# Score matmuls issued one by one, a work list for projections, and output tiles of the last head group moved forward, in a fused attention and gated-MLP kernel

## The chip, the cores and the metric

The kernel runs on one core of a Trainium2 chip. The metric is device time in microseconds (us) of one execution; lower is better. Executions agree within about 0.2%, so an effect of 1 us in 1309 needs both repeated timing and the trace of one profiled execution. I name the engines as the profile does: PE (TensorE), PEld (its weight loads), ACT (ScalarE), DVE (VectorE), POOL (GpSimd), SP (SyncE, which issues the DMAs).

## The reference, cut to what matters

```python
xn = layernorm(x)                                   # x: 2048 x 512
q  = (xn @ wq) split in 32 heads of 128             # 512 x 4096
p  = softmax(q @ k_cache.T * 128**-0.5)             # per head 2048 x 2048
s  = concat_heads(p @ v_cache) @ wo                 # 4096 x 512
g  = silu(((relu(xn @ W_gate)) * (xn @ W_up)) @ W_down)
return x + s * g                                    # bf16 in and out
```

## The kernel before

A *block* is one head and 512 queries; there are 128 blocks (32 heads x 4). A block has 8 *steps*. In a step PE makes two score tiles (keys x queries, 128 x 512), ACT takes the exponential of both in one instruction, and three steps later PE uses the result as weights of eight value matmuls (129 columns: 128 values and one column that sums the softmax denominator). PSUM holds three pairs of banks for scores and projections (the ring) and two accumulator banks for the values. After a block's last value matmul DVE normalises the two banks (the *norm*), and DMA transposes the result for the output projection.

In the first step of a block PE also makes one query projection for the next head and one *output tile*: a 128 x 512 tile of the output projection of the previous group of 4 heads. Output tiles are summed in `s_acc`; the last group's 16 *final tiles* come after the loop and go straight into the result.

```python
def emit_S_pair(gp):                     # two scores, then the exp
    ...
    s = ring_acquire()
    for tt in range(2):
        ins = pe.matmul(ps_r[:, 2 * s + tt, :], KT_sb[h % 2][:, t * 128:(t + 1) * 128],
                        QT_sb[h % 2][:, qs], start=True, stop=True)
    ...
def emit_norm_bank(b, bank, pvtok):
    ob = b % NON                                     # NON = 16 buffers, one group
    _wait(dve, pvtok)
    if bank == 0 and b % (G * QB) == 0 and g >= 1:
        _wait(dve, t_tok(g - 1))                     # all transposes of the group before
    ...                                              # 1 reciprocal, 2 scalings per bank
    sp.dma_start_transpose(OT_store[...], Onorm[ob][:, j, :])   # 4 per block
...
for step in range(LAG, TOTP + LAG):
    emit_S_pair(gp)                                  # step gp
    if pq == 0:
        emit_M(hq + 1, Qq, op_item)                  # projection and at most one output tile
    emit_PV_pair(gq)                                 # values of step gp - 3: 8 matmuls
while oproj_queue: ...                               # what is left of group 6
for n in range(NT):                                  # 16 final tiles of group 7
    if n == 0:
        _wait(pe, t_tok(gL))
    ...                                              # 4 matmuls
    dve.tensor_tensor(fin_tmp[fb][:], ps_r[:, bank, 0:D], g_sb[:, n, :], ALU.mult)
    dve.tensor_tensor(x_sb[:, n, :], x_sb[:, n, :], fin_tmp[fb][:], ALU.add)
    ...                                              # stores
```

The softmax here doesn't subtract the row's maximum and nothing guards it: scores larger than these inputs give would overflow.

Of the kernel before, what the change touches and what calls it, by code (L numbers as in the profile page):

```python
# [5 lines left out]
BF16 = mybir.dt.bfloat16  # L6
# [45 lines left out]
def bass_recurrent_scan__mha_block_cached__glu_gated_reglu__prompt_kernel(  # L52
# [18 lines left out]
    NQ = 512  # L71
# [32 lines left out]
    with ExitStack() as es:  # L104
# [9 lines left out]
        def newsem(unit=1):  # L114
            _cnt[0] += 1
            return _Sem(es.enter_context(nc.semaphore(f"sem{_cnt[0]}")), unit)
# [47 lines left out]
        sem_out = newsem(16)  # L164
        sem_pool = newsem()
# [28 lines left out]
        with nc.Block() as block:  # L194

            @block.tensor
            def _(_pe_eng):
# [298 lines left out]
                oproj_queue = []  # L496
                bcount = [0]
                OPROJ_DELAY = 2

# [5 lines left out]
                def emit_M(h_qp, Q_qp, op_item):  # L505
                    do_qp = h_qp is not None and h_qp < H and (h_qp, Q_qp) not in qt_ready
                    if not do_qp and op_item is None:
                        return
                    s = ring_acquire()
                    toks = []  # L510
                    if do_qp:
                        toks.append(emit_qp(h_qp, Q_qp, 2 * s))
                    if op_item is not None:
                        g_, n_ = op_item
                        toks.append(emit_oproj_tile(g_, n_, 2 * s + 1))
                    ring_tok[s] = toks
# [59 lines left out]
                def emit_S_pair(gp):  # L576
                    b, h, Q, p = blk_of(gp)
                    qs = slice(Q * NQ, (Q + 1) * NQ)
                    if p == 0:
                        if (h, Q) not in qt_ready:  # L580
                            emit_M(h, Q, None)
                        _wait(pe, qt_ready[(h, Q)])
                        if Q == 0:
                            _wait(pe, kt_tok(h))
                    s = ring_acquire()
                    ins = None
                    for tt in range(2):
                        t = 2 * p + tt
                        ins = pe.matmul(ps_r[:, 2 * s + tt, :], KT_sb[h % 2][:, t * 128:(t + 1) * 128],  # L589
                                        QT_sb[h % 2][:, qs], start=True, stop=True)  # L590
# [11 lines left out]
                def emit_norm_bank(b, bank, pvtok):  # L602
# [10 lines left out]
                    for jj in range(2):  # L613
# [7 lines left out]
                        )  # L621
                    _wait(sp, tok)
                    if bank == 0 and b % (G * QB) == 0 and g >= 2:
                        _wait(sp, opg_tok.get(g - 2))
                    for jj in range(2):
                        j = 2 * bank + jj
                        sem_t[g % 2].sig(
# [7 lines left out]
                def emit_PV_pair(gp):  # L635
# [3 lines left out]
                    if p == 0:  # L639
                        if gp == 0:  # L640
                            _wait(pe, tok_pool)
                        if Q == 0:
                            _wait(pe, v_tok(h))
                    pe.wait_ge(sem_exp.h, gp + 1)
                    for tt in range(2):
                        t = 2 * p + tt
                        for j in range(4):
                            bank = j // 2
                            if t == 0 and j % 2 == 0:
                                _wait(pe, norm_tok[b - 1][bank] if b >= 1 else acc_free[bank])  # L650
                            o_ap = ps_acc[:, bank, (j % 2) * 256:(j % 2) * 256 + VW]
                            ins = pe.matmul(o_ap, PT[pb][:, tt, j * 128:(j + 1) * 128], V_sb[vb][:, t, :],  # L652
                                            start=(t == 0 and j % 2 == 0), stop=(t == KT - 1 and j % 2 == 1))
                            if t == KT - 1 and j == 1:
                                tx = sem_pv.sig(ins)
                            if t == KT - 1 and j == 3:
                                ty = sem_pv.sig(ins)
                    if p == NP - 1:
# [6 lines left out]
                        g, hh = divmod(h, G)  # L665
                        if hh == G - 1 and Q == QB - 1 and g < NG - 1:
                            for n in range(NT):
                                oproj_queue.append((bcount[0] + OPROJ_DELAY, g, n))

# [5 lines left out]
                for Q in range(QB):  # L675
                    emit_M(0, Q, None)
                sp_head_start(0)
                for gp in range(LAG):
                    emit_S_pair(gp)
                emit_down(QB - 1, hlast)  # L680
                glu_done_tok = sem_g.cur()
                if NG == 1:
                    for n in range(NT):
                        base_done[n] = None

                for step in range(LAG, TOTP + LAG):
                    gp = step
                    if gp < TOTP:
                        b, h, Q, p = blk_of(gp)
                        if p == 0 and Q == 0:  # L690
                            sp_head_start(h)
                        emit_S_pair(gp)
                    gq = step - LAG
                    if gq >= 0:
                        bq, hq, Qq, pq = blk_of(gq)
                        if pq == 0:
                            bcount[0] += 1
                            op_item = None
                            if oproj_queue and oproj_queue[0][0] <= bcount[0]:
                                _, g_, n_ = oproj_queue.pop(0)  # L700
                                op_item = (g_, n_)
                            emit_M(hq + 1, Qq, op_item)
                        emit_PV_pair(gq)

                while oproj_queue:
                    _, g_, n_ = oproj_queue.pop(0)
                    emit_M(None, None, (g_, n_))
                gL = NG - 1
                NFT = len(fin_tmp)
                fin_free = [None] * NFT  # L710
                fin_tok = {}
                chunk_start = [0]
                cur_slot = [None, []]

                for n in range(NT):
                    fb = n % NFT
                    if n % 2 == 0:
                        s = ring_acquire()
                        slot_toks = []
                    bank = 2 * s + (n % 2)  # L720
                    if n == 0:
                        _wait(pe, t_tok(gL))
                        _wait(pe, wo_tok(gL))
                    ins = None
# [3 lines left out]
                    otok = sem_op.sig(ins)  # L728
                    _wait(dve, otok)
                    _wait(dve, fin_free[fb])  # L730
                    mtok = sem_opa.sig(dve.tensor_tensor(fin_tmp[fb][:], ps_r[:, bank, 0:D], g_sb[:, n, :], ALU.mult))  # L731
                    slot_toks.append(mtok)
                    ring_tok[s] = list(slot_toks)
                    _wait(dve, mtok)
                    if n == 0:
                        _wait(dve, base_done.get(NT - 1))
# [38 lines left out]
```

## Time and profile before

The kernel before took 1308.88 us (median of 3). These lines are from the page of its profiled execution: the span, PE's busy time, and the chain of waits that ended last.

```profile
span 1309.6 us, 27449 instructions
PE 1281.4 (98%) x11744; PEld 838.4 (64%) x11964; DVE 442.6 (34%) x1190; ACT 1000.7 (76%) x1107; POOL 11.5 (1%) x23
...
PE 93%; DVE 3%; issue 2%; DMA 1%; SPq 0%; ACTq 0%; DVEq 0%
```

PE is the bound nearly everywhere. "98% busy" alone would not show it, since ends of matmuls are modelled; start-to-start intervals of the trace do. Means over complete steps without a projection, between 345 and 1240 us, in ns:

| | two scores | eight values | step |
|---|---|---|---|
| before | 216.7, 215.8 | 56.7, 56.7, 56.7, 56.7, 60.8, 55.9, 56.7, 57.5 | 890.0 |

The next lines, of DVE's timeline, give the first reciprocal of a norm, thus the end of a block (start, duration, instruction, and in brackets the idle time before it and what ended it). They are blocks 122 to 127.

```profile
1239.68 0.17 DVE L610 RECIPROCAL rz_sb<-ps_acc 128x2 f32<-128x2 f32 x1 [4.43 <-PE ps_acc L652]
...
1248.52 0.17 DVE L610 RECIPROCAL rz_sb<-ps_acc 128x2 f32<-128x2 f32 x1 [4.43 <-PE ps_acc L652]
...
1256.79 0.17 DVE L610 RECIPROCAL rz_sb<-ps_acc 128x2 f32<-128x2 f32 x1 [4.68 <-PE ps_acc L652]
...
1265.06 0.17 DVE L610 RECIPROCAL rz_sb<-ps_acc 128x2 f32<-128x2 f32 x1 [4.68 <-PE ps_acc L652]
...
1273.32 0.17 DVE L610 RECIPROCAL rz_sb<-ps_acc 128x2 f32<-128x2 f32 x1 [4.68 <-PE ps_acc L652]
...
1280.30 0.17 DVE L610 RECIPROCAL rz_sb<-ps_acc 128x2 f32<-128x2 f32 x1 [3.39 <-PE ps_acc L652]
```

A full block takes 8.85 us: 8 x 0.890 plus 8 matmuls of 0.216. The last four have no projection (no next head). Blocks 124 to 126 take 8.27 us, although 8 x 0.890 + 4 x 0.216 is only 7.98: with so little between two blocks' values, PE waits for the norm. (Block 127 ends 6.98 us after block 126, because its last three steps have no scores to make.) The view of waits has it (waiter, what it waited for, total, times, longest).

```profile
PEld ps_acc L652 <- DVE Onorm L617: 6.1, 21, 0.5
```

The tail, first PE's timeline, then the busy times by window (stretch, length, then busy time and instructions of each engine, PE's granted clock, DMA share, GB/s), then DVE's last instructions:

```profile
1278.38 2.00 PE L652 MATMUL ps_acc<-V_sb,PT 128*128 128x129 bf16 x32
1280.43 0.81 PE L545 MATMUL ps_r<-Wo_sb,OT_store 128*128 128x512 bf16 x3
1287.25 11.58 PE L726 MATMUL ps_r<-Wo_sb,OT_store 128*128 128x512 bf16 x40 [6.01 <-issue]
```

```profile
1281.30:1287.20 5.90, 0.00 (x0) 0.00 (x0) 2.51 (x5) 0.00 (x0) 0.00 (x0) 0.91 0.10 22
1287.20:1293.20 6.00, 5.95 (x15) 2.20 (x16) 2.87 (x5) 0.00 (x0) 0.00 (x0) 0.52 0.00 0
1293.20:1307.60 14.40, 10.76 (x50) 4.70 (x48) 13.88 (x28) 0.00 (x0) 0.00 (x0) 0.96 0.39 132
```

```profile
1306.08 0.43 DVE L737 TENSOR_TENSOR x_sb<-x_sb,fin_tmp 128x512 bf16<-128x512 bf16 x1
1306.42 0.68 DVE L731 TENSOR_TENSOR fin_tmp<-ps_r,g_sb 128x512 bf16<-128x512 f32 x1
...
1307.14 0.42 DVE L737 TENSOR_TENSOR x_sb<-x_sb,fin_tmp 128x512 bf16<-128x512 bf16 x1
```

Three things follow one another: PE stands still for 6.01 us (the profile names no releaser, "issue", but the kernel waits there for the last head's DMA transposes, and the trace has the last of them landed at 1287.16), then it runs at about half clock (0.52) for 6 us, then DVE is busy 13.88 of 14.40 us at 1.06 us per tile. From the last value matmul's start (1280.16) to the end are 29.5 us.

### The profile page before, as it was taken

The numbers are of one execution on the slowest core, as the hardware profiler recorded it, in microseconds if no ns is written. First come the engines' busy times: TensorE is split into PE (matmuls) and PEld (weight loads), VectorE is DVE, ScalarE is ACT, GpSimd is POOL, SyncE is SP. The second block draws the span as 40 slices with busy tenths as digits, with TensorE's granted clock in tenths as the row PEclk, the third lists the DMA queues.
The fourth block names the chain that finished last, engine by engine and source line by source line (L and its number), as shares of the span: only waits on it lengthen the run. The fifth ranks groups of instructions, "written<-read, shape, count | busy, mean of one in ns | idle before, by whom it ended". The sixth has DMA issues, their size and how long they took to land.

```text
span 1309.6 us, 27449 instructions
## 1 busy us (share of the span) xinstructions
PE 1281.4 (98%) x11744; PEld 838.4 (64%) x11964; DVE 442.6 (34%) x1190; ACT 1000.7 (76%) x1107; POOL 11.5 (1%) x23
## 2 busy tenths in 40 slices
PE   9999999999999999999999999999999999999996
PEld 3444466666666666666666666666666666666663
DVE  6333322222332332233233233223323323344546
ACT  3322389998888888888888888888888888888880
POOL 2000000000000000000000000000000000000000
PEclk9999999999999999999999999999999999999998
DMA  8500112232222322232221222222223222212202
GB/s 254 116 1 1 21 37 51 46 61 41 45 51 53 70 51 52 53 68 53 52 52 40 57 42 51 52 70 53 52 52 69 51 53 53 50 44 43 48 18 70
DMA packets 251575, 71.82 MB, mean 55 GB/s; under 512 B 238400, under 2 KB 251456, under 8 KB 251456
## 3 DMA queue, kind: packets, MB, share of 16 engines
q1 hardware_dynamic: 250640, 69.55, 25.4%
q8 instruction: 95, 1.56, 0.5%
q10 hardware_dynamic: 816, 0.52, 0.1%
q14 instruction: 24, 0.20, 0.0%
HBM read 32.77 MB, written 2.10 MB: 27 GB/s over the span
## 4 chain that ended last, share of the span: by engine, by line
PE 93%; DVE 3%; issue 2%; DMA 1%; SPq 0%; ACTq 0%; DVEq 0%
PE ps_acc L652 36%; PE ps_r L589 32%; PE ps_r L524 7%; PE ps_r L545 7%; PE ps_r L423 4%; PE ps_r L419 4%; PE ps_acc L456 4%; DVE Onorm L617 2%; DVE fin_tmp L731 1%; DMA Wu_sb<-in_B_W_up_dram 1%; PE ps_r L726 0%; DVE rz_sb L610 0%; SPq L628 0%; DMA OT_store<-Onorm 0%; ACTq L224 0%
## 5 line engine op out<-in xcount | busy, mean ns | idle before, releaser
L597 ACT ACTIVATE PT<-ps_r 128x1024 bf16<-128x1024 f32 x1024 | 952.3, 1054 | 172.8 <-PE ps_r L589 172.8
L652 PEld LDWEIGHTS ps_acc<-V_sb,PT 128*128 128x128 bf16 x8192 | 551.8, 98 | 247.9 <-DVE Onorm L617 6.1
L652 PE MATMUL ps_acc<-V_sb,PT 128*128 128x129 bf16 x8192 | 640.3, 221 | 2.5 <-DVE Onorm L617 0.4
L589 PE MATMUL ps_r<-QT_sb,KT_sb 128*128 128x512 bf16 x1844 | 565.5, 379 | 10.6
L610 DVE RECIPROCAL rz_sb<-ps_acc 128x2 f32<-128x2 f32 x256 | 42.2, 165 | 736.9 <-PE ps_acc L652 710.6
L589 PEld LDWEIGHTS ps_r<-QT_sb,KT_sb 128*128 128x128 bf16 x2048 | 159.3, 98 | 1.1 <-DVE QT_sb L535 0.4
L617 DVE TENSOR_SCALAR Onorm<-ps_acc,rz_sb 128x128 bf16<-128x128 f32 x512 | 156.1, 347 | 9.2
L524 PE MATMUL ps_r<-xnT,Wq_sb 128*128 128x512 bf16 x511 | 130.8, 379 | 0.1
L545 PE MATMUL ps_r<-Wo_sb,OT_store 128*128 128x512 bf16 x447 | 114.8, 379 | 0.1
L524 PEld LDWEIGHTS ps_r<-xnT,Wq_sb 128*128 128x128 bf16 x512 | 50.1, 98 | 60.5
L535 DVE CAST QT_sb<-ps_r 128x512 bf16<-128x512 f32 x128 | 87.2, 681 | 0.7 <-PE ps_r L524 0.7
L545 PEld LDWEIGHTS ps_r<-Wo_sb,OT_store 128*128 128x128 bf16 x448 | 43.8, 98 | 52.6 <-DMA OT_store<-Onorm 0.2
L429 ACT ACTIVATE gr_sb<-ps_r 128x512 bf16<-128x512 f32 x56 | 33.4, 596 | 56.2 <-PE ps_r L419 53.5
L558 DVE TENSOR_TENSOR s_acc<-s_acc,ps_r 128x512 f32<-128x512 f32 x96 | 65.9, 687 | 12.3
L419 PE MATMUL ps_r<-xnT,Wg_sb 128*128 128x512 bf16 x220 | 57.7, 384 | 1.0 <-DMA Wu_sb<-in_B_W_up_dram 0.8
L423 PE MATMUL ps_r<-xnT,Wu_sb 128*128 128x512 bf16 x219 | 57.8, 384 | 0.3
L435 DVE TENSOR_TENSOR hT<-gr_sb,ps_r 128x512 bf16<-128x512 bf16 x56 | 38.5, 687 | 50.4 <-PE ps_r L423 46.6
L456 PE MATMUL ps_acc<-Wd_sb,hT 128*128 128x512 bf16 x220 | 48.8, 379 | 0.2
L419 PEld LDWEIGHTS ps_r<-xnT,Wg_sb 128*128 128x128 bf16 x224 | 22.0, 99 | 27.8 <-issue 1.1
L423 PEld LDWEIGHTS ps_r<-xnT,Wu_sb 128*128 128x128 bf16 x224 | 22.1, 99 | 27.1 <-issue 1.1
L462 ACT ACTIVATE sig_sb<-ps_acc 128x512 f32<-128x512 f32 x16 | 9.6, 597 | 38.8 <-PE ps_acc L456 36.4
L456 PEld LDWEIGHTS ps_acc<-Wd_sb,hT 128*128 128x128 bf16 x224 | 21.9, 98 | 26.5
(33 smaller groups left out, 128.1 us busy)
## 6 DMA issues: line engine op xcount, KB each, us to landing
V_sb<-in_A_v_cache_dram SPq DMA_DIRECT2D x32, 512.0 KB, 5.0
OT_store<-Onorm SPq DMA_TRANSPOSE x512, 2.4
Wq_sb<-in_A_wq_dram SPq DMA_DIRECT2D x32, 128.0 KB, 2.7
Wo_sb<-in_A_wo_dram SPq DMA_DIRECT2D x8, 512.0 KB, 4.2
Wd_sb<-in_B_W_down_dram SPq DMA_DIRECT2D x1, 1792.0 KB, 13.5
Wg_sb<-in_B_W_gate_dram SPq DMA_DIRECT2D x2, 768.0 KB, 9.4
Wu_sb<-in_B_W_up_dram SPq DMA_DIRECT2D x2, 768.0 KB, 10.4
x_sb<-in_A_x_dram SPq DMA_DIRECT2D x3, 512.0 KB, 10.8
```

The costliest lines, as they stand in the source:

```text
L419: ins = pe.matmul(ps_r[:, gb, :], Wg_sb[:, c, fs], xnT[:, c, qs], start=(c == 0), stop=(c == DC - 1))
L423: ins = pe.matmul(ps_r[:, gb + 1, :], Wu_sb[:, c, fs], xnT[:, c, qs], start=(c == 0), stop=(c == DC - 1))
L456: ins = pe.matmul(ps_acc[:, jb, 0:D], hT[par][:, fc, j * 128:(j + 1) * 128], Wd_sb[:, fc, :], start=(fc == 0), stop=(fc == FC - 1))
L524: ins = pe.matmul(ps_r[:, bank, :], Wq_sb[b][:, c, :], xnT[:, c, qs], start=(c == 0), stop=(c == DC - 1))
L535: etok = sem_qpe.sig(dve.tensor_copy(QT_sb[b][:, qs], ps_r[:, bank, :]))
L545: ins = pe.matmul(ps_r[:, bank, 0:D], OT_store[g % 2][:, hh, n * 128:(n + 1) * 128], Wo_sb[g % 2][:, hh, :], start=(hh == 0), stop=(hh == ...
L558: dve.tensor_tensor(s_acc[:, n, :], s_acc[:, n, :], ps_r[:, bank, 0:D], ALU.add)
L589: ins = pe.matmul(ps_r[:, 2 * s + tt, :], KT_sb[h % 2][:, t * 128:(t + 1) * 128], QT_sb[h % 2][:, qs], start=True, stop=True)
L597: act.activation(PT[pb][:], ps_r[:, 2 * s:2 * s + 2, :], ACTF.Exp, scale=scale)
L610: rztok = sem_rz.sig(dve.reciprocal(rz_sb[:, bank, :, :], z_ap))
L617: dve.tensor_scalar(Onorm[ob][:, j, :], ps_acc[:, bank, base:base + Dh], rz_sb[:, bank, jj, :], None, op0=ALU.mult,)
L652: ins = pe.matmul(o_ap, PT[pb][:, tt, j * 128:(j + 1) * 128], V_sb[vb][:, t, :], start=(t == 0 and j % 2 == 0), stop=(t == KT - 1 and j % ...
```

## The change

It has three parts. (1) *Singles*: outside the first step, a step is now score, four values, score, four values, instead of two scores and eight values. (2) A *plan* by block and step replaces the queue of output tiles; for the main part it puts the same work in the same places. (3) *The last blocks*: what was left of group 6 goes into blocks 124 and 125; of the last group, final tiles 0 to 7 go into blocks 126 and 127 ("two blocks behind their heads": queries of block 124 are done in block 126); and the last block is transposed on PE, with ACT copying the result, so that only 8 final tiles come after the loop. The core of the diff, with cuts:

```diff
-                emit_S_pair(gp)
+                open_S_pair(gp)
+                emit_S_tile(gp, 0)
+                if items:
+                    emit_S_tile(gp, 1)
+            if items:
+                emit_M(items)
-                emit_PV_pair(gq)
+            emit_PV_tile(gq, 0)
+            if gp < TOTP and not items:
+                emit_S_tile(gp, 1)
+            emit_PV_tile(gq, 1)
 ...
+        for g in range(NG - 1):
+            for n in range(NT):
+                b = (g + 1) * GB + 1 + n
+                if b < LB:                           # LB = 124
+                    plan[(b, 0)].append((emit_oproj_tile, g, n))
+                else:
+                    k = n - (LB - (g + 1) * GB - 1)
+                    plan.setdefault((LB + k // 4, 4 * (k // 2 % 2)), []).append((emit_oproj_tile, g, n))
+        for Q in range(QB - 2):
+            for j in range(4):
+                plan.setdefault((LB + 2 + Q, 4 * (j // 2)), []).append((emit_final_tile, 4 * Q + j))
 ...
+                    if b == NBLK - 1:
+                        emit_last_transposes(hh, Q, ob, bank, tok)   # PE transposes, later
+                        return tok
 ...
-        for n in range(NT):                          # 16 final tiles
+        for n in range(NT - 8, NT - 4, 2):
+            emit_M([(emit_final_tile, n), (emit_final_tile, n + 1)])
+        flush_last_transposes()                      # 4 PE transposes, 2 ACT copies
+        for n in range(NT - 4, NT, 2):
+            emit_M([(emit_final_tile, n), (emit_final_tile, n + 1)])
```

More of the change, by code (lines that the diff above doesn't have):

```diff
@@ L164, in bass_recurrent_scan__mha_block_cached__glu_gated_reglu__prompt_kernel @@
         sem_out = newsem(16)
+        sem_tl = [newsem(16) for _ in range(QB)]
+        sem_ptr = newsem()
+        sem_otc = newsem()
         sem_pool = newsem()
@@ L495, in _ @@
                 opg_tok = {}
-                oproj_queue = []
-                bcount = [0]
-                OPROJ_DELAY = 2
                 def blk_of(gp):
@@ L503, in blk_of, with emit_M @@
                     return b, h, Q, p
-                def emit_M(h_qp, Q_qp, op_item):
-                    do_qp = h_qp is not None and h_qp < H and (h_qp, Q_qp) not in qt_ready
-                    if not do_qp and op_item is None:
-                        return
+                def emit_M(items):
                     s = ring_acquire()
-                    toks = []
-                    if do_qp:
-                        toks.append(emit_qp(h_qp, Q_qp, 2 * s))
-                    if op_item is not None:
-                        g_, n_ = op_item
-                        toks.append(emit_oproj_tile(g_, n_, 2 * s + 1))
+                    toks = [fn(*args, 2 * s + k) for k, (fn, *args) in enumerate(items)]
                     ring_tok[s] = toks
@@ L574, in emit_base, with open_S_pair @@
                     )
-                def emit_S_pair(gp):
+                s_slot = {}
+                def open_S_pair(gp):
                     b, h, Q, p = blk_of(gp)
-                    qs = slice(Q * NQ, (Q + 1) * NQ)
                     if p == 0:
-                        if (h, Q) not in qt_ready:
-                            emit_M(h, Q, None)
                         _wait(pe, qt_ready[(h, Q)])
@@ L584, in emit_S_pair, with emit_S_tile @@
                             _wait(pe, kt_tok(h))
-                    s = ring_acquire()
-                    ins = None
-                    for tt in range(2):
-                        t = 2 * p + tt
-                        ins = pe.matmul(ps_r[:, 2 * s + tt, :], KT_sb[h % 2][:, t * 128:(t + 1) * 128],
-                                        QT_sb[h % 2][:, qs], start=True, stop=True)
+                    s_slot[gp] = ring_acquire()
+                def emit_S_tile(gp, tt):
+                    b, h, Q, p = blk_of(gp)
+                    qs = slice(Q * NQ, (Q + 1) * NQ)
+                    s = s_slot[gp]
+                    t = 2 * p + tt
+                    ins = pe.matmul(ps_r[:, 2 * s + tt, :], KT_sb[h % 2][:, t * 128:(t + 1) * 128],
+                                    QT_sb[h % 2][:, qs], start=True, stop=True)
+                    if tt == 0:
+                        return
                     stok = sem_s.sig(ins)
@@ L624, in emit_norm_bank @@
                         _wait(sp, opg_tok.get(g - 2))
+                    tsem = sem_t[g % 2] if g < NG - 1 else sem_tl[Q]
                     for jj in range(2):
                         j = 2 * bank + jj
-                        sem_t[g % 2].sig(
+                        tsem.sig(
                             sp.dma_start_transpose(
@@ L633, in emit_norm_bank, with emit_last_transposes, flush_last_transposes, emit_PV_tile @@
                     return tok
-                def emit_PV_pair(gp):
+                last_ot = {}
+                def emit_last_transposes(hh, Q, ob, bank, tok):
+                    pending_last.append((hh, Q, ob, bank, tok))
+                def flush_last_transposes():
+                    s = ring_acquire()
+                    for k, (hh, Q, ob, bank, tok) in enumerate(pending_last):
+                        tp_ps = ps_r[:, 2 * s + k, :].bitcast(BF16)
+                        _wait(pe, tok)
+                        ins = None
+                        for jj in range(2):
+                            j = 2 * bank + jj
+                            ins = pe.transpose(tp_ps[:, jj * 128:(jj + 1) * 128], Onorm[ob][:, j, :], ident[:])
+                        ptok = sem_ptr.sig(ins)
+                        _wait(act, ptok)
+                        c0 = Q * NQ + bank * 256
+                        last_ot[bank] = sem_otc.sig(
+                            act.copy(OT_store[(NG - 1) % 2][:, hh, c0:c0 + 256], tp_ps[:, 0:256])
+                        )
+                    ring_tok[s] = list(last_ot.values())
+                pending_last = []
+                def emit_PV_tile(gp, tt):
                     b, h, Q, p = blk_of(gp)
@@ L638, in emit_PV_pair @@
                     vb = h % 2
-                    if p == 0:
-                        if gp == 0:
-                            _wait(pe, tok_pool)
-                        if Q == 0:
-                            _wait(pe, v_tok(h))
-                    pe.wait_ge(sem_exp.h, gp + 1)
-                    for tt in range(2):
-                        t = 2 * p + tt
-                        for j in range(4):
-                            bank = j // 2
-                            if t == 0 and j % 2 == 0:
-                                _wait(pe, norm_tok[b - 1][bank] if b >= 1 else acc_free[bank])
-                            o_ap = ps_acc[:, bank, (j % 2) * 256:(j % 2) * 256 + VW]
-                            ins = pe.matmul(o_ap, PT[pb][:, tt, j * 128:(j + 1) * 128], V_sb[vb][:, t, :],
-                                            start=(t == 0 and j % 2 == 0), stop=(t == KT - 1 and j % 2 == 1))
-                            if t == KT - 1 and j == 1:
-                                tx = sem_pv.sig(ins)
-                            if t == KT - 1 and j == 3:
-                                ty = sem_pv.sig(ins)
-                    if p == NP - 1:
+                    if tt == 0:
+                        if p == 0:
+                            if gp == 0:
+                                _wait(pe, tok_pool)
+                            if Q == 0:
+                                _wait(pe, v_tok(h))
+                        pe.wait_ge(sem_exp.h, gp + 1)
+                    t = 2 * p + tt
+                    for j in range(4):
+                        bank = j // 2
+                        if t == 0 and j % 2 == 0:
+                            _wait(pe, norm_tok[b - 1][bank] if b >= 1 else acc_free[bank])
+                        o_ap = ps_acc[:, bank, (j % 2) * 256:(j % 2) * 256 + VW]
+                        ins = pe.matmul(o_ap, PT[pb][:, tt, j * 128:(j + 1) * 128], V_sb[vb][:, t, :],
+                                        start=(t == 0 and j % 2 == 0), stop=(t == KT - 1 and j % 2 == 1))
+                        if t == KT - 1 and j == 1:
+                            tx = sem_pv.sig(ins)
+                        if t == KT - 1 and j == 3:
+                            ty = sem_pv.sig(ins)
+                    if t == KT - 1:
                         if Q == QB - 1 and h + 2 < H:
@@ L664, in emit_PV_pair @@
                         norm_tok[b] = (ntx, nty)
-                        g, hh = divmod(h, G)
-                        if hh == G - 1 and Q == QB - 1 and g < NG - 1:
-                            for n in range(NT):
-                                oproj_queue.append((bcount[0] + OPROJ_DELAY, g, n))
                 def sp_head_start(h):
@@ L673, in sp_head_start, with emit_final_tile @@
                         issue_kt(h + 1)
-                for Q in range(QB):
-                    emit_M(0, Q, None)
-                sp_head_start(0)
-                for gp in range(LAG):
-                    emit_S_pair(gp)
-                emit_down(QB - 1, hlast)
-                glu_done_tok = sem_g.cur()
-                if NG == 1:
-                    for n in range(NT):
-                        base_done[n] = None
-                for step in range(LAG, TOTP + LAG):
-                    gp = step
-                    if gp < TOTP:
-                        b, h, Q, p = blk_of(gp)
-                        if p == 0 and Q == 0:
-                            sp_head_start(h)
-                        emit_S_pair(gp)
-                    gq = step - LAG
-                    if gq >= 0:
-                        bq, hq, Qq, pq = blk_of(gq)
-                        if pq == 0:
-                            bcount[0] += 1
-                            op_item = None
-                            if oproj_queue and oproj_queue[0][0] <= bcount[0]:
-                                _, g_, n_ = oproj_queue.pop(0)
-                                op_item = (g_, n_)
-                            emit_M(hq + 1, Qq, op_item)
-                        emit_PV_pair(gq)
-                while oproj_queue:
-                    _, g_, n_ = oproj_queue.pop(0)
-                    emit_M(None, None, (g_, n_))
-                gL = NG - 1
                 NFT = len(fin_tmp)
                 fin_free = [None] * NFT
-                fin_tok = {}
-                chunk_start = [0]
-                cur_slot = [None, []]
-                for n in range(NT):
-                    fb = n % NFT
-                    if n % 2 == 0:
-                        s = ring_acquire()
-                        slot_toks = []
-                    bank = 2 * s + (n % 2)
+                fin_cnt = [0]
+                gL = NG - 1
+                def emit_final_tile(n, bank):
+                    Q, j = divmod(n, 4)
                     if n == 0:
-                        _wait(pe, t_tok(gL))
                         _wait(pe, wo_tok(gL))
+                    if j == 0:
+                        _wait(pe, (sem_tl[Q], sem_tl[Q].n))
+                    if Q == QB - 1:
+                        _wait(pe, last_ot[j // 2])
                     ins = None
@@ L728, in _ @@
                     otok = sem_op.sig(ins)
+                    fb = fin_cnt[0] % NFT
+                    fin_cnt[0] += 1
                     _wait(dve, otok)
                     _wait(dve, fin_free[fb])
-                    mtok = sem_opa.sig(dve.tensor_tensor(fin_tmp[fb][:], ps_r[:, bank, 0:D], g_sb[:, n, :], ALU.mult))
-                    slot_toks.append(mtok)
-                    ring_tok[s] = list(slot_toks)
+                    mtok = sem_opa.sig(
+                        dve.tensor_tensor(fin_tmp[fb][:], ps_r[:, bank, 0:D], g_sb[:, n, :], ALU.mult))
@@ L734, in _ @@
                     _wait(dve, mtok)
                     if n == 0:
-                        _wait(dve, base_done.get(NT - 1))
-                    ftok = sem_opa.sig(dve.tensor_tensor(x_sb[:, n, :], x_sb[:, n, :], fin_tmp[fb][:], ALU.add))
+                        _wait(dve, base_done[NT - 1])
+                    ftok = sem_opa.sig(
+                        dve.tensor_tensor(x_sb[:, n, :], x_sb[:, n, :], fin_tmp[fb][:], ALU.add))
                     fin_free[fb] = ftok
-                    fin_tok[n] = ftok
@@ L740, in _ @@
-                    rem = NT - 1 - n
-                    csz = 4 if rem >= 4 else (2 if rem >= 2 else 1)
-                    if (n + 1 - chunk_start[0]) >= csz:
+                    if Q == QB - 1 or j % 2 == 1:
+                        n0 = n if Q == QB - 1 else n - 1
                         _wait(sp, ftok)
-                        sem_out.sig(sp.dma_start(out_t[:, chunk_start[0]:n + 1, :], x_sb[:, chunk_start[0]:n + 1, :]))
-                        chunk_start[0] = n + 1
+                        sem_out.sig(sp.dma_start(out_t[:, n0:n + 1, :], x_sb[:, n0:n + 1, :]))
@@ new lines, in emit_final_tile @@
+                    return mtok
+                plan = {}
+                for b in range(NBLK):
+                    h, Q = divmod(b, QB)
+                    if h + 1 < H:
+                        plan[(b, 0)] = [(emit_qp, h + 1, Q)]
+                GB = G * QB
+                LB = NBLK - QB
+                for g in range(NG - 1):
[6 more added lines that the diff above has]
+                            plan.setdefault((LB + k // 4, 4 * (k // 2 % 2)), []).append((emit_oproj_tile, g, n))
@@ new lines, in _ @@
+                for Q in range(QB - 2):
+                    for j in range(4):
+                        plan.setdefault((LB + 2 + Q, 4 * (j // 2)), []).append((emit_final_tile, 4 * Q + j))
+                for Q in range(0, QB, 2):
+                    emit_M([(emit_qp, 0, Q), (emit_qp, 0, Q + 1)])
+                sp_head_start(0)
+                for gp in range(LAG):
+                    open_S_pair(gp)
+                    emit_S_tile(gp, 0)
+                    emit_S_tile(gp, 1)
+                emit_down(QB - 1, hlast)
@@ new lines, in _ @@
+                glu_done_tok = sem_g.cur()
+                for step in range(LAG, TOTP + LAG):
+                    gp = step
+                    gq = step - LAG
+                    bq, hq, Qq, pq = blk_of(gq)
+                    items = plan.pop((bq, pq), None)
+                    if gp < TOTP:
+                        b, h, Q, p = blk_of(gp)
+                        if p == 0 and Q == 0:
+                            sp_head_start(h)
+                        open_S_pair(gp)
+                        emit_S_tile(gp, 0)
+                        if items:
[4 more added lines that the diff above has]
+                    if gp < TOTP and not items:
+                        emit_S_tile(gp, 1)
+                    emit_PV_tile(gq, 1)
@@ L746, in _ @@
+                assert not plan
+                for n in range(NT - 8, NT - 4, 2):
[3 more added lines that the diff above has]
+                    emit_M([(emit_final_tile, n), (emit_final_tile, n + 1)])
                 sp.wait_ge(sem_out.h, sem_out.n)
```

## The prediction

> **What bounds it now.** TensorE, nearly everywhere: the page has PE 98% busy, the chain of waits gives PE 93% of the span. Ends of matmuls are modelled, so I used start-to-start intervals from the trace. Between 300 and 1240 us a score, projection or output matmul takes 0.216 us, a value matmul 0.057 us; so a step (2 scores, 8 values) is 0.89 us and a block (8 steps plus 8 projection/output matmuls, 1.73 us) 8.85 us. The observed block period is 8.85 us. The Trainium skill ("TensorE: Matmul & The Clock Gate", Back-to-back issue gap) states N/2.4 + 2.5 ns, i.e. 215.8 and 56.3 ns; the trace shows 215.8 and mostly 56.7. The steady state has no hole. ScalarE needs 7.44 of 8.85 us per block: not the bound.
>
> Not bound by TensorE is the end (timeline):
> - The last value matmul starts at 1280.2 us, the last queued output tile ends by 1281.3. Then PE idles 6.0 us for the last head's four DMA transposes (landed 1287.2).
> - After that hole output matmuls are 0.426 us apart until 1293.1 us, twice the normal: the clock fell. The same page (HAM clock gate) says an idle window halves it; this trace agrees.
> - Then VectorE bounds: 0.69 + 0.42 us of work, 1.06 us per tile, 16 tiles, ending at 1307.56; the last store ends the span at 1309.6.
> - The last four blocks have no projection: period 8.27 us, with a 0.28 us PE stall each for the norm (waits view: 21 such, 6.1 us).
>
> **What the change does.**
> 1. Scores singly: same instructions, other order; nearly nothing. Possible gain: the fifth interval in a group of 8 values is 60.8 instead of 56.7 ns; if that went, 4 ns x 900 steps = 3.7 us. I count 1 us.
> 2. Projections in a list: same places up to block 123, no change; paired at the start, no change (no hole there).
> 3. Last four blocks: work moves from the tail into them, old output tiles 11-15 to blocks 124/125, final tiles 0-7 to 126/127. Blocks 124, 126, 127 get four 0.86 us tiles each (and lose the stall), 125 one. From block 124's start at 1248.9: 10.6 + 8.3 + 10.6 + 8.9 puts the last value matmul at about 1287.3 instead of 1280.2 (+7.1). A head's transposes land 6.2 us after its block, so final tiles a block later should not wait.
> 4. Tail: the hole goes. Tiles 8-11 (3.5 us PE) cover the norm, then PE transposes and two ScalarE copies (estimate 0.4 us each, from the 0.60 us ACTIVATE of 512 columns). VectorE then bounds: norm 1.6 us, 8 tiles x 1.06 = 8.5, ending near 1297.4; plus 2.0 for the last store: 1299.5.
>
> Tail after the last value matmul: 29.4 now, about 12.1 after. Net -17.3 + 7.1 = -10.2 us, minus 1 for point 1: about 1298 us.
>
> **Predicted: 1298 us, range 1293 to 1302. Faster by over 2%: 0.02; within 2%: 0.97; slower: 0.01.**
>
> **Signs in the profile.** Period of blocks 20-120 still 8.85 us (8.82 to 8.86). Blocks 124, 126, 127 about 10.6 us apart. No PE gap over 1 us after the last value matmul, full clock to the end. VectorE at 1.06 us per tile for eight tiles at the end.
>
> **What would make it wrong.** A value group of four with a score between costing or saving some ns (repeated 900 times: 10 ns are 9 us); VectorE falling behind in block 124 (four tiles x 2.1 us of work, in order before the norm), stalling PE; a wait for transposes at the first final tiles; each exp's start, 0.23 us later, becoming a wait.

## The result, and the profile after

The changed kernel took 1299.91 us (median of 4, 1299.02 to 1301.79) against 1309.16 for the kernel before beside it. Ratio 0.9931, 95% interval 0.9914 to 0.9949. (Ratios are the mean time of one kernel's runs over that of the other's of the same rounds, so not quite the ratio of the medians quoted.) All outputs are right. The page's lines:

```profile
span 1298.6 us, 27683 instructions
PE 1287.6 (99%) x11968; PEld 835.3 (64%) x11968; DVE 442.5 (34%) x1190; ACT 1001.6 (77%) x1109; POOL 11.5 (1%) x23
...
PE 93%; DVE 3%; SPq 2%; DMA 1%; issue 0%; ACT 0%; DVEq 0%
```

The ends of the same blocks, 122 to 127:

```profile
1238.68 0.17 DVE L605 RECIPROCAL rz_sb<-ps_acc 128x2 f32<-128x2 f32 x1 [4.42 <-PE ps_acc L675]
...
1247.52 0.17 DVE L605 RECIPROCAL rz_sb<-ps_acc 128x2 f32<-128x2 f32 x1 [4.42 <-PE ps_acc L675]
...
1258.32 0.16 DVE L605 RECIPROCAL rz_sb<-ps_acc 128x2 f32<-128x2 f32 x1
...
1266.56 0.17 DVE L605 RECIPROCAL rz_sb<-ps_acc 128x2 f32<-128x2 f32 x1 [4.67 <-PE ps_acc L675]
...
1277.28 0.17 DVE L605 RECIPROCAL rz_sb<-ps_acc 128x2 f32<-128x2 f32 x1 [1.66 <-PE ps_acc L675]
...
1286.56 0.17 DVE L605 RECIPROCAL rz_sb<-ps_acc 128x2 f32<-128x2 f32 x1 [0.37 <-PE ps_acc L675]
```

Blocks 124 to 127 now take 10.80, 8.24, 10.72 and 9.28 us. The reciprocal at 1258.32 has no idle time before it: DVE came to it straight from the four output tiles of block 124, about 0.2 us late. The tail, by PE's timeline and by window:

```profile
1284.64 2.00 PE L675 MATMUL ps_acc<-V_sb,PT 128*128 128x129 bf16 x32
1286.47 3.62 PE L709 MATMUL ps_r<-Wo_sb,OT_store 128*128 128x512 bf16 x16
1289.93 0.39 PE L647 MATMUL ps_r<-ident,Onorm 128*128 128x128 bf16 x4
1290.75 3.61 PE L709 MATMUL ps_r<-Wo_sb,OT_store 128*128 128x512 bf16 x16 [0.44 <-ACT OT_store L652]
```

```profile
1286.50:1290.70 4.20, 3.81 (x23) 1.75 (x20) 4.00 (x11) 0.46 (x2) 0.00 (x0) 1.00 0.18 62
1290.70:1294.40 3.70, 3.61 (x16) 1.50 (x16) 3.56 (x9) 0.18 (x1) 0.00 (x0) 1.00 0.45 151
1294.40:1296.60 2.20, 0.00 (x0) 0.00 (x0) 2.11 (x5) 0.00 (x0) 0.00 (x0) 1.00 0.40 136
```

The hole is 0.44 us, the clock stays at 1.00, and DVE is the bound for 8 tiles instead of 16. I cut each trace at three instants: the first value matmul, the norm of block 123, and the start of the last value matmul. In us:

| profiled execution | start to first value | first value to norm 123 | norm 123 to last value | tail | span |
|---|---|---|---|---|---|
| before | 162.14 | 1086.38 | 31.63 | 29.46 | 1309.6 |
| after | 160.53 | 1086.98 | 38.90 | 12.21 | 1298.6 |
| difference | -1.61 | +0.60 | +7.27 | -17.25 | -11.0 |

The first column is chance: the code there is the same but for the pairing of four projections, where neither trace has a hole. In the profiled execution of the kernel before, the first four gate matmuls took 1.66 us, in the other 1.02: PE was still at the lower clock. One of the experiments (the changed kernel with pairs) also started late, at 162.06, and its first four gate matmuls took 1.71 us; all others lie between 160.35 and 160.88. Without this column the difference is 9.4 us, in line with the timing (9.2 us between the medians).

The second column is the surprise: +0.60 us where I had hoped for -1. Intervals say that singles work: the 60.8 ns interval is gone, a step is 1.7 ns shorter (means, ns):

| | score, 4 values | score, 4 values | step |
|---|---|---|---|
| after | 216.3; 56.7, 57.1, 57.0, 57.1 | 216.2; 56.7, 57.1, 57.1, 57.1 | 888.3 |

So a block takes 8.835 us instead of 8.847 (medians of 20 to 100), about 1.5 us over the run. What takes it back? Two lines from the waits (the 28.7 us are DVE's idle time, most of which it would otherwise have spent waiting for PE), and three from the timeline where group 7 starts (block 112; the block before it ended at 1140.69):

```profile
DVE rz_sb L605 <- DMA OT_store<-Onorm: 28.7, 4, 7.4
...
PEld ps_acc L675 <- DVE Onorm L612: 7.0, 21, 0.5
```

```profile
1141.54 6.39 SPq L627 DMA_TRANSPOSE OT_store<-Onorm  x4
...
1150.91 0.17 DVE L605 RECIPROCAL rz_sb<-ps_acc 128x2 f32<-128x2 f32 x1 [7.26 <-DMA OT_store<-Onorm]
...
1152.51 0.52 PE L675 MATMUL ps_acc<-V_sb,PT 128*128 128x129 bf16 x6 [0.36 <-DVE Onorm L612]
```

At the first block of a group DVE waits for all transposes of the group before, the last of which were issued only one block earlier. The trace has the next head's loads in front of them on SP's queue: keys, then values, then the four transposes. The last was issued 6.0 us after its block's end and landed 10.1 us after it; in the last four blocks of the kernel before, where no heads are loaded, the last landed 6.9 to 7.8 us after the block's end. Part of the delay is the queue, part is that this one transpose took 4.1 us to land where most take 2.3 or 2.4. The norm started late, and the values of the next block waited for it. The seven group starts of this trace bear it out: where the norm was late (groups 1, 3, 4, 7), the last transpose had landed 9.5 to 10.1 us after its block's end; at the other three it had landed after 8.3 to 8.6 us, less than the 8.84 of a block. A norm that is up to about 0.6 us late costs nothing: at group 3 of the kernel before, one block took 9.44 us and the next 8.27, together no more than two full blocks. Comparing block periods around each group start, this cost 2.6 us in the profiled execution of the changed kernel (groups 1, 3, 4 and 7) and 0.6 us in that of the kernel before (group 7 alone).

### The profile page after: what moved, and what is told of

The parts are those of the page before. It is cut to its first block, busy times and chain, and to the rows that moved or that the text cites. A ratio compares the mean times of both kernels' runs of the same rounds, so it can differ in the third digit from the quotient of the medians.

```text
span 1298.6 us, 27683 instructions
## 1 busy us (share of the span) xinstructions
PE 1287.6 (99%) x11968; PEld 835.3 (64%) x11968; DVE 442.5 (34%) x1190; ACT 1001.6 (77%) x1109; POOL 11.5 (1%) x23
## 4 chain that ended last, share of the span: by engine, by line
PE 93%; DVE 3%; SPq 2%; DMA 1%; issue 0%; ACT 0%; DVEq 0%
PE ps_acc L675 35%; PE ps_r L582 32%; PE ps_r L515 7%; PE ps_r L536 7%; PE ps_r L422 4%; PE ps_acc L459 4%; PE ps_r L426 4%; DVE Onorm L612 2%; SPq L627 2%; PE ps_r L709 1%; DMA OT_store<-Onorm 1%; DVE rz_sb L605 0%; DMA x_sb<-in_A_x_dram 0%; DVE stats L313 0%; DVE s_acc L561 0%
## 5 line engine op out<-in xcount | busy, mean ns | idle before, releaser
L675 PE MATMUL ps_acc<-V_sb,PT 128*128 128x129 bf16 x8192 | 784.2, 221 | 3.3 <-DVE Onorm L612 1.6
L675 PEld LDWEIGHTS ps_acc<-V_sb,PT 128*128 128x128 bf16 x8192 | 623.1, 98 | 249.3 <-DVE Onorm L612 7.0
L582 PE MATMUL ps_r<-QT_sb,KT_sb 128*128 128x512 bf16 x2048 | 755.1, 380 | 0.0
L582 PEld LDWEIGHTS ps_r<-QT_sb,KT_sb 128*128 128x128 bf16 x2048 | 195.4, 98 | 1.1 <-DVE QT_sb L526 0.4
L515 PEld LDWEIGHTS ps_r<-xnT,Wq_sb 128*128 128x128 bf16 x512 | 49.8, 97 | 60.8 <-ACT PT L592 24.2
```

The costliest lines, as they stand in the source:

```text
L515: ins = pe.matmul(ps_r[:, bank, :], Wq_sb[b][:, c, :], xnT[:, c, qs], start=(c == 0), stop=(c == DC - 1))
L675: ins = pe.matmul(o_ap, PT[pb][:, tt, j * 128:(j + 1) * 128], V_sb[vb][:, t, :], start=(t == 0 and j % 2 == 0), stop=(t == KT - 1 and j % ...
```

## The experiments

Eleven kernels were run against the kernel before, each timed 4 or 5 times. "Stretch" is from the first value matmul to the norm of block 123. Theory A: the gain is the last blocks and the tail, as predicted, and singles are worth about 1 us that the late norms hide. Theory B: singles carry the gain.

### Singles alone, and the change without singles

The first edit put single scores into the kernel before; the second took them out of the changed kernel:

```diff
# changed kernel, pairs again
                 emit_S_tile(gp, 0)
-                if items:
-                    emit_S_tile(gp, 1)
+                emit_S_tile(gp, 1)
 ...
-            if gp < TOTP and not items:
-                emit_S_tile(gp, 1)
```

> The kernel before, with only the scores issued singly between groups of four values (pairs kept in the step with the projections); tail and last blocks as before. Theory A (the gain is all in the last blocks and the tail): time within 2 us of the kernel before (1307 to 1310); block period 8.84 instead of 8.85 us, because the 60.8 ns interval goes, worth up to 1.9 us over the run, partly or wholly lost again at group starts where the norm waits for DMA transposes. Theory B (singles carry the gain): about 1300 us. The tail after the last value matmul stays 29.4 us under both.

> The changed kernel, with scores issued in pairs again. Theory A: within 2 us of the changed kernel (1298 to 1302), block period back to 8.85 us, last-block periods 10.8, 8.3, 10.7, 9.3 us and a tail of 12.2 us as in the changed kernel. Theory B (singles carry the gain): about 1308 us.

Singles alone: 1308.05 us against 1309.85, ratio 0.9987 (0.9974 to 1.0), block 8.835 us, stretch 1085.10 us, tail 28.53. The change with pairs: 1300.65 us, ratio 0.9924 (0.9910 to 0.9937), block 8.847 us, stretch 1086.33, tail 12.20. Theory B falls: the gain stays when singles go. The tail of the first was 0.9 us shorter than expected. By its trace the final matmuls start 7.09 us after the last value matmul, as in the kernel before, but the half clock ends at 10.0 us instead of 12.9. So the half clock lasted differently long in these two runs; no run shows what sets it.

### The two halves of the tail, each alone

In one run only the transposes of the last block went to PE, with all 16 final tiles after the loop; in the other the final tiles stayed in the blocks, and the transposes went back to DMA.

```diff
# kernel before, PE transposes only
+                    if b == NBLK - 1:
+                        emit_last_transposes(hh, Q, ob, bank, tok)
+                        return tok
 ...
+                flush_last_transposes()
                 for n in range(NT):
# changed kernel, DMA transposes
-                    if b == NBLK - 1:
-                        emit_last_transposes(hh, Q, ob, bank, tok)
-                        return tok
 ...
-                flush_last_transposes()
```

> The kernel before, with only the last head's transposes moved from DMA to TensorE plus two ScalarE copies; all 16 final tiles still after the loop. My sum: last value matmul at the same distance, the 6.0 us hole shrinks to about 2 us, no half clock after it, VectorE bound for 16 tiles x 1.06 us: tail 29.4 to about 23.3 us, so 6 us faster (about 1303). Rival (the moved final tiles carry nearly all of the gain, the hole is only where they would have waited for VectorE anyway): under 3 us faster.

> The changed kernel, with the last head's transposes back on DMA; final tiles 0 to 7 still in blocks 126 and 127. My sum: tiles 8 to 11 end 3.5 us after the last value matmul, the transposes land about 6.9 us after it, so PE waits some 3.3 us instead of about 1, tiles 12 to 15 then take 4.5 us of VectorE: tail 12.2 to about 14.5 us, 2 to 3 us slower than the changed kernel (about 1302). Rival (PE transposes carry most of the gain): 6 us slower, about 1306.

PE's timeline in the first of them, and then in the second:

```profile
1278.38 1.03 PE L547 MATMUL ps_r<-Wo_sb,OT_store 128*128 128x512 bf16 x4
1279.43 0.27 PE L653 MATMUL ps_r<-ident,Onorm 128*128 128x128 bf16 x2
1280.06 0.28 PE L653 MATMUL ps_r<-ident,Onorm 128*128 128x128 bf16 x2 [0.36 <-DVE Onorm L619]
1281.01 13.97 PE L757 MATMUL ps_r<-Wo_sb,OT_store 128*128 128x512 bf16 x64 [0.67 <-ACT OT_store L658]
```

```profile
1284.86 3.62 PE L704 MATMUL ps_r<-Wo_sb,OT_store 128*128 128x512 bf16 x16
1291.95 3.61 PE L704 MATMUL ps_r<-Wo_sb,OT_store 128*128 128x512 bf16 x16 [3.46 <-DMA OT_store<-Onorm]
```

| | norm 123 to last value | tail | sum | ratio to before (95%) |
|---|---|---|---|---|
| before | 31.63 | 29.46 | 61.09 | 1 |
| PE transposes only | 31.63 | 22.86 | 54.49 | 0.9948 (0.9936 to 0.9961) |
| moved tiles only (DMA transposes) | 38.95 | 14.58 | 53.53 | 0.9941 (0.9928 to 0.9953) |
| both (the change) | 38.90 | 12.21 | 51.11 | 0.9931 (0.9914 to 0.9949) |

The first rival ("under 3 us") and the second ("6 us slower") fall. By the traces the halves save 6.6 and 7.6 us alone and 10.0 together: they overlap, since both do away with the hole, one by shortening the wait, the other by having work to put in it. The 6.6 us of the first half have two parts: the final matmuls start 2.69 us after the last value matmul instead of 7.09 (4.4 us), and from there DVE needs 18.1 us instead of 20.3, since PE is not at half clock (2.2 us). The 3.46 us hole with moved tiles cost no clock: the 16 matmuls after it are 0.216 us apart, as the 3.61 us show.

### The late norms, with singles and with pairs

Here the normalised heads get 32 buffers, DVE waits for the group before the last, and the output tiles start one block later, so that no first tile waits either. The second run is the same with pairs.

```diff
-    NON = G * QB
+    NON = 2 * G * QB
 ...
-                    if bank == 0 and b % (G * QB) == 0 and g >= 1:
-                        _wait(dve, t_tok(g - 1))
+                    if bank == 0 and b % (G * QB) == 0 and g >= 2:
+                        _wait(dve, t_tok(g - 2))
 ...
-                b = (g + 1) * GB + 1 + n
+                b = (g + 1) * GB + 2 + n
```

> The changed kernel, with 32 normalised-head buffers instead of 16 (so VectorE at a group's first block waits for the transposes of two groups before, not of the group just ended), and each group's output tiles one block later. Theory (the late starts of the norms at blocks 16, 48, 64 and 112, up to 1.4 us each, are waits for DMA transposes delayed by the next head's loads): no such late start, and the stretch from the first value matmul to the norm of block 123 falls from 1086.98 and 1085.10 us (the two profiles of singles in this order) to about 1084.5; 0.6 to 2 us faster than the changed kernel. Rival (the wait is for something else, or the late landing only moves to the first output tile): no change.

> The kernel of the run above, but with scores in pairs. Theory (singles are worth 12 ns per block in the steady state, 8.847 to 8.835 us, and only the random late transposes hid it): 1.3 to 1.6 us slower than the run above in the stretch from the first value matmul to the norm of block 123. Rival (singles are worth nothing): no difference in that stretch.

The waits of the first of the two, all that name the norm's tiles; the wait for DMA is gone:

```profile
DVE rz_sb L605 <- PE ps_acc L675: 723.3, 127, 6.1
...
PEld ps_acc L675 <- DVE Onorm L612: 4.8, 17, 0.3
```

With singles: 1297.64 us, ratio 0.9910 (0.9897 to 0.9924), stretch 1083.79 us. With pairs: 1299.00 us, ratio 0.9920 (0.9908 to 0.9932), stretch 1085.23. So the late norms are waits for the transposes (the three edits were not tried one by one, but the wait is gone and blocks 20 to 120 all take 8.834 to 8.837 us). Taking them away shortens the stretch by 3.2 us against the profiled execution of the changed kernel, the one that lost most, and by 1.3 against that of singles alone; the last blocks give 0.4 us back (39.26 instead of 38.90), as two old output tiles move into block 125 instead of one. Without the late norms the worth of singles stands out in the two traces: 1.44 us. The timed intervals of the two overlap, so that figure rests on the traces and on the constant 12 ns per block.

### Filling the hole at the norm

The waits above (32 buffers, singles) leave 17 stalls of about 0.28 us, in the blocks with a projection but no output tile. PE has to wait for the *second* bank's norm. The edit does first what needs only the first bank, and then borrows the first score of the next step, which single issue made possible:

```diff
+            if pq == 0 and len(items) == 1 and gp + 1 < TOTP:
+                emit_PV_tile(gq, 0, (0,))            # values of bank 0, both score tiles
+                emit_PV_tile(gq, 1, (0,))
+                open_S_pair(gp + 1)
+                emit_S_tile(gp + 1, 0)
+                emit_PV_tile(gq, 0, (1,))            # values of bank 1
+                emit_PV_tile(gq, 1, (1,))
+                continue
             emit_PV_tile(gq, 0)
```

> The changed kernel, with another order in the first step of each block that has one projection only: after it, the values of the first accumulator bank for both score tiles, then the first score of the next step, then the values of the second bank. Theory (the 0.27 us hole there is the wait for the norm of the second bank, and a score of 0.216 us plus two values of 0.057 us fill it): blocks 1 to 15 go from 8.254 to about 7.98 us, 17 blocks and block 125 in all, 4.6 us faster (about 1295.3). Rival (ScalarE, at 7.44 us per block with exps started later, becomes the wait): under 2 us faster.

The same line of its waits, against 7.0 us and 21 times in the changed kernel:

```profile
PEld ps_acc L677 <- DVE Onorm L612: 1.7, 5, 0.5
```

It took 1294.26 us, ratio 0.9885 (0.9870 to 0.9900). Blocks 1 to 15 went from 8.254 to 7.975 us, and 8 x 0.888 + 4 x 0.216 is 7.97: no hole is left in them, so ACT did not become the wait.

### A faster tail, two ways

The first way put the transposes one pair of tiles earlier, and every second of the last 8 additions on POOL. The second kept the earlier transposes, but let ACT bring final tiles 8 to 14 out of PSUM as bf16, so that DVE multiplies and adds from SBUF. Both also get four buffers for the product instead of two (not shown).

```diff
# first way
-                    ftok = sem_opa.sig(dve.tensor_tensor(x_sb[...], x_sb[...], fin_tmp[fb][:], ALU.add))
+                    eng = pool if n >= NT - 8 and n % 2 == 0 else dve
+                    ftok = (...).sig(eng.tensor_tensor(x_sb[...], x_sb[...], fin_tmp[fb][:], ALU.add))
# second way, tiles 8 to 14
-                    dve.tensor_tensor(fin_tmp[fb][:], ps_r[:, bank, 0:D], g_sb[:, n, :], ALU.mult)
+                    act.copy(fin_tmp[fb][:], ps_r[:, bank, 0:D])
+                    dve.tensor_tensor(fin_tmp[fb][:], fin_tmp[fb][:], g_sb[:, n, :], ALU.mult)
```

> The changed kernel, with the last head's transposes one pair of final tiles earlier and every second of the last 8 final additions on GpSimd. Theory (the tail is bound by VectorE at 1.06 us per tile, next by the TensorE chain): tail 12.2 to about 10.9 us, 1.3 us faster. Rival (GpSimd's additions are slow or slow VectorE down): no gain, or slower.

> The changed kernel with that tail alone: tail about 11 us instead of 12.2. Against the GpSimd version of the tail (12.4 us) this tells whether it was the place of the additions (GpSimd beside VectorE) or the earlier transposes that failed there.

The timeline of one pair of tiles on the first way, and of one tile on the second:

```profile
1288.00 1.28 DVE L719 TENSOR_TENSOR fin_tmp<-ps_r,g_sb 128x512 bf16<-128x512 f32 x2
1288.76 1.15 POOL L726 TENSOR_TENSOR x_sb<-x_sb,fin_tmp 128x512 bf16<-128x512 bf16 x1 [0.96 <-DVE fin_tmp L719]
1289.31 0.88 DVE L726 TENSOR_TENSOR x_sb<-x_sb,fin_tmp 128x512 bf16<-128x512 bf16 x1
```

```profile
1288.75 0.58 ACT L719 CAST fin_tmp<-ps_r 128x512 bf16<-128x512 f32 x1 [0.28 <-PE ps_r L710]
1288.97 0.43 DVE L732 TENSOR_TENSOR x_sb<-x_sb,fin_tmp 128x512 bf16<-128x512 bf16 x1
1289.37 0.43 DVE L722 TENSOR_TENSOR fin_tmp<-fin_tmp,g_sb 128x512 bf16<-128x512 bf16 x1
```

The first way failed: tail 12.43 us, none gained (1299.57 us, ratio 0.9922). DVE's addition, 0.42 us elsewhere, took 0.88 us beside POOL's, and ended 0.28 us after POOL's did; the multiplications, with one operand in PSUM, kept their pace. That agrees with the Trainium skill ("SBUF — State Buffer", Who interferes with whom): a DVE instruction with two SBUF inputs contends with a GpSimd instruction that reads SBUF. The rival in the expectation was right. The second way gave a tail of 11.13 us (1297.18 us, ratio 0.9904, 0.9890 to 0.9919), so it was the place of the additions that failed, not the earlier transposes. PE, 0.86 us per tile, is then the bound of the tail.

### All together

> The changed kernel with the two successful edits together: the later output tiles with 32 buffers, and the reordered first step that fills the hole. If the two gains are of different places they add: first value matmul to norm of block 123 about 1079.3 us (1083.8 with the first edit alone, minus 17 x 0.27), no late norms, tail 12.2 us: about 1292 to 1293 us. If filling only hides what the late transposes cost anyway, it stays at the 1294 us of the second edit alone.

> The kernel of the run above, with another tail: the transposes one pair of final tiles earlier, and for final tiles 8 to 14 ScalarE copies the product out of PSUM as bf16, so that VectorE multiplies and adds from SBUF. If VectorE's 1.06 us per tile bounds the tail, tail about 11 us and 1 us faster than the run above; the next bound is the chain of TensorE, 0.86 us per tile.

The two edits of the main loop together: 1292.85 us, ratio 0.9870 (0.9855 to 0.9885), stretch 1078.86 us, close to the 1079.3 us forecast for gains that add. This is the only wait of that trace that names the norm's tiles; PE waits for no norm any more:

```profile
DVE rz_sb L605 <- PE ps_acc L677: 718.4, 127, 5.9
```

With the ACT tail as well: 1291.54 us, ratio 0.9864 (0.9848 to 0.9881), tail 11.13. It beats both kernels, by 1.4% the one before.

## Why the prediction was right

The time was within the range (1299.9 in 1293 to 1302), and the sums for the last blocks and the tail held; the step that did not hold is the main loop (point 2). One thing was luck: my base, 1309.6 us, was the span of an execution that started 1.6 us late and was timed at 1311.41. That it lies near the timed median (1308.88 to 1309.85) is because the late start and the 1.8 us that the span left out (1311.41 - 1309.6) nearly cancel.

1. *What bounds the kernel.* Right: where PE had no hole, nothing moved but the 1.7 ns per step. The Trainium skill ("TensorE: Matmul & The Clock Gate", Back-to-back issue gap) gave a formula for the gap, 215.8 and 56.3 ns, from which "no hole to fill" followed; the page itself keeps it for isolated matmuls (see the end), but the trace agreed with it (215.8 and 56.7 ns).
2. *Singles.* "I count 1 us" for the 60.8 ns interval: it went, and singles were worth 1.44 us with the late norms taken away. In the changed kernel as profiled the late norms hid it, so the stretch grew by 0.60 us. I had written that projections in a list mean "no change" up to block 123, and had not seen that group starts wait on DMA. By the profiled executions (+0.60 instead of -1) this is the main part of the 1.9 us by which I was too low; with one trace each, and losses that vary as much as they do, that share is not shown for the timed runs. Whether single issue itself makes late norms likelier is open: kernels with singles and the old wait lost 0.4 to 2.6 us that way, those with pairs 0 to 0.6, one trace each.
3. *Last blocks.* +7.1 predicted, +7.27 measured. A single sign was off: block 127 took 9.28 us, where my sum had 8.9 and my signs "about 10.6". The risk I named, DVE behind in block 124, came true with about 0.2 us. One premise was off: I wrote that a head's transposes land 6.2 us after its block; from the block's end it is 6.9 to 7.8 us in the kernel before, and those of block 124 in the changed kernel took 8.6 us (landed 1266.93). PE stood still 0.16 us for them, until the first final tile at 1267.07: a near miss. (The view of waits names ACT, which had ended at 1266.72; the weight load started 0.104 us after the landing, and 0.104 and 0.105 us after it in the two other runs where PE stood still there, those with DMA transposes and with additions on POOL.)
4. *Tail.* 12.1 us predicted, 12.21 measured; PE's gap 0.44 us, full clock, DVE 1.06 us per tile, as foretold.
5. *The half clock.* The skill's section on the HAM clock gate says that an idle window, given as about 3.4 us, halves the clock. The hole of 6.01 us did (0.52 granted, matmuls 0.426 us apart), that of 3.46 us did not. No run here shows how long a hole may be.

The prediction also lacked something in its search: some 4.6 us lay in 17 holes of the changed kernel. I had listed such holes (waits view, 21 of them, 6.1 us in all), but under the last four blocks, where only 4 of the 21 lie; the change left those of the first blocks alone.

## What to carry to other kernels

Cost a change by start-to-start intervals and by the instants between which work moves: here -17.25 in the tail and +7.27 in the blocks that took the work, each within 0.2 us of the sum done beforehand. Reordering a saturated engine brought little by itself here (1.4 us), but the finer unit of issue (a single score) could then be put exactly where a hole was, and filled it. A wait for everything of the group before lasts as long as the slowest and latest member of that group; here twice the buffers, with a wait for the group before that one, took it off the path.

## What the Trainium skill lacked or had wrong

- "TensorE: Matmul & The Clock Gate", Back-to-back issue gap, says that a stream of weight loads and matmuls runs at about 81 ns (128 columns) and 131 ns (512 columns), and that N/2.4 + 2.5 holds for isolated matmuls only. Here every matmul has its own weight load, and the sustained intervals were 56.7 ns (129 columns) and 215.8 ns (512): the formula, not the sustained figures.
- The same page has nothing on the 60.8 ns interval, always the fifth in eight value matmuls that follow a pair of scores and gone with groups of four. No run explains it.
- Its Part 4 says that a PE transpose of 128 x 128 takes about 275 ns in a kernel and that the full clock does not engage for it. Here four in a row, right after dense matmuls, started 56 ns apart at a granted clock of 1.00, each shown as 219 ns long (ends are modelled). Whether transposes alone would bring up the full clock, no run shows.
- "DMA: Bandwidth & Descriptors", DMA Transpose, gives no time for a small transpose between SBUF tiles: 128 x 128 took a median of 2.4 us from issue to landing, and SP issued them 1.27 us apart. In the changed kernel 160 of 508 took over 3 us, the longest 6.15; one of 4.1 us fell beside the next head's loads, another (issued at 1262.84) where no head was being loaded. Why is open.
- "SBUF — State Buffer" was right on GpSimd and VectorE (0.42 us became 0.88). No page has the time of a GpSimd addition of this size and type: 128 x 512 bf16 took 1.15 us here, always beside one of VectorE's, nearly three times VectorE's 0.42 alone (spans on GpSimd are rough).
